# Fourier mixing with experts: fewer expert pieces a step, and the relu between the two copies of the inverse's second stage

## The chip, the cores and the metric

The kernel runs on one core of one Trainium2 chip. The metric is the device time of one execution in microseconds (us).

## What is computed

For each of 8 sequences of 3136 rows with 256 channels: a Fourier transform along the rows, a complex matrix product with soft thresholding, the inverse transform, and then, on the 128 rows with the highest gate score, an expert of two dense layers whose result is added. All of it is float32. Cut to the core:

```python
X = np.fft.rfft(x, axis=1)
Yr = Xr @ w_r - Xi @ w_i + b_r
Yi = Xr @ w_i + Xi @ w_r + b_i
Y* = np.sign(Y*) * np.maximum(np.abs(Y*) - 0.01, 0.0)      # real and imaginary part
y = np.fft.irfft(Y, n=3136, axis=1)
scores = y @ w_gate
for b in range(8):
    top = np.argpartition(-scores[b], 128)[:128]
    ye = np.maximum(y[b, top] @ w1, 0) @ w2
    out[b, top] = y[b, top] + sigmoid(scores[b, top])[:, None] * ye
```

## The kernel before, in words

The transform of 3136 = 98 x 32 is done in two stages each way. The work is cut into T = 100 units (sequence b, group g of frequencies), and one loop over the step t (line 788) writes the order of all engines out by hand; nothing is rescheduled later, each engine runs its list in order. In step t stand, in this order:

- `s2` (forward stage two) of unit t + 1: TensorE products into the bank `px`, on ScalarE the rounded copy `Xh` (L500), on VectorE the rest `Xl` (L501).
- `pair`: one product group `s1` (forward stage one, L440) or `s1i` (inverse stage one, L632) of other sequences, with ScalarE's copy of its result (`at` L443, `ot` L634).
- `turn("pe", "da")`: one move of the router, which finds the 128 rows by eight rounds of counting; its product of a round (L260) writes into the bank `pca`. Placing the rows (L300 to L334) follows.
- `spectral` of unit t (L503): six products into `pcb[:, D:]` (the sum product), ScalarE's copy `ks` (L515), GpSimd's `kb` (ks plus bias, L517), twelve products into `py`, and VectorE's addition of `kb` onto `py` (L521).
- Expert pieces. `ffns` holds two Python generators, `fetch` (L698, gathers the 128 rows) and `ffn` (L707: `prepare` with two transposes and VectorE's and ScalarE's work on gate and rows, 16 first-layer products in 8 pieces of two, 8 combining products in 8 pieces). One `tick` moves each generator by one piece. The number a step is set at line 820.
- A second `pair`, where there is one.
- `s2i` of unit t - 1 (L531, inverse stage two): eight products into `pca[:, :D]` and `pcb[:, :D]` (L549), then for each of the two a ScalarE copy into `ct` (L559) and a VectorE product with the gate's weights that sums up (`junk`, `Csc`, L561). ScalarE copies `pca` while VectorE reads `pcb`, then they change over.
- `shrink` of unit t (L524): ScalarE's relu `r1` of `py` (L526), VectorE's `Y` from `py` and `r1` (L528). `py` has one buffer, so the twelve products of the next step wait for `Y`; the next step's sum product writes the bank `pcb`, from which the second copy reads.

Experts of sequences 0 to 4 may run inside the loop from step 40 on, once the sequence's output is stored; those of 5, 6 and 7 come at step 98 and after. Behind the loop, a list of turns (`work` L855, `fill` L655) mixes the last router's rounds, the last `s1i`, the experts that are left and filler products (L664) that compute nothing.

Of the kernel before, what the change touches and what calls it, by code (L numbers as in the profile page):

```python
# [111 lines left out]
def fourier_moe(ctx: ExitStack, tc: tile.TileContext, x, w_r, w_i, b_r, b_i, wg, w1, w2,  # L112
# [46 lines left out]
    def ld(out, src):  # L159
        nc.sync.dma_start(out=out, in_=src)  # L160
# [35 lines left out]
    def consts_g(k):  # L196
        if k < 3:
            s = slice(8 * k, 8 * k + 8)
            ld(g_sb[:, s, :], t_g[:, s, :])
        else:  # L200
            ld(gt_sb, t_gt)
# [206 lines left out]
    def ld_x(b, i):  # L408
        if i % 2:
            return  # L410
        k = i // 2
        t = (cvs if b < 2 and k > 1 else xts)[k % 2]
        xt[b, k] = t.rearrange("p (h c) d -> p h c d", h=2)
        ld(t.rearrange("p c d -> p (c d)"), x[b, k])
# [106 lines left out]
        nc.vector.tensor_tensor(out=py[:r], in0=py[:r], in1=kb[:r], op=ALU.add)  # L521
        return py, r

    def shrink(b, g, py, r):  # L524
        r1 = pool.tile([128, 2, D], F32, name="r1", bufs=RB)
        nc.scalar.activation(out=r1[:r], in_=py[:r], func=AF.Relu, bias=m2l[:r], scale=1.0)  # L526
        y = pool.tile([128, 2, D], F32, name="Y", bufs=YB)
        nc.vector.scalar_tensor_tensor(out=y[:r], in0=py[:r], scalar=0.0, in1=r1[:r], op0=ALU.min, op1=ALU.add)  # L528
        Y[b, g] = y

    def s2i(b, g):  # L531
        for k in (b, b + 1 if g == G - 1 else b):
            if k not in Cs:
                Cs[k] = Csd[k]
                Csc[k] = pool.tile([128, 32], F32, name="Csc")
                nc.vector.memset(Csc[k][:, NJ - 1:], 0.0)
        if g == G - 1:
            ct[b, g] = pool.tile([128, 2, D], F32, name="ct2", bufs=1)
        elif g % 4 == 0:
            ct[b] = pool.tile([128, 8, D], F32, name="ct", bufs=2)  # L540
        y = Y.pop((b, g))
        p = [t[:, :D] for t in (pca, pcb)]
        if (b, g) == units[T - 1]:
            p = [ps.tile([128, 2, 2 * D], F32, name="px", bufs=1)[:, 0, :D], pcb[:, :D]]
        if g < G - 1:
            for c in range(2):
                for q in range(2):
                    for a in range(2):
                        nc.tensor.matmul(p[q][64 * a:64 * a + 64], gi_sb[64 * q:64 * q + 64, g, c, 64 * a:64 * a + 64], y[64 * q:64 * q + 64, c, :],  # L549
                                         start=(c == 0), stop=(c == 1))  # L550
        else:
            for c in range(2):
                for k in range(2):
                    nc.tensor.matmul(p[k][:64], gti_sb[64 * k:64 * k + 64, c, :], y[64 * k:64 * k + 64, c, :], start=(c == 0), stop=(c == 1))
        o = 2 * (g % 4)
        t = ct[b, g] if g == G - 1 else ct[b]
        for k in (1, 0):
            r, bk, col = (128, b, 2 * g + k) if g < G - 1 else (64, b + k, NJ - 1)
            nc.scalar.copy(out=t[:r, o + 1 - k, :], in_=p[1 - k][:r])  # L559
            junk = pool.tile([128, D], F32, name="junk", bufs=1)  # L560
            nc.vector.tensor_tensor_reduce(out=junk[:r], in0=p[k][:r], in1=wgb[:r], scale=1.0, scalar=0.0,  # L561
                                           op0=ALU.mult, op1=ALU.add, accum_out=Csc[bk][:r, col:col + 1])
        if g == G - 1:
            def store():
                for k in range(2):
                    for q in range(2):
                        ld(Cs[b + k][q, 48] if b + k < B - 1 else Cs[b + k][(N1 - 1) * q], t[q:64:2, k, :])
            stores.append(store)
        elif b == B - 1 and g in (3, 7, 10, 11):
            def store():  # L570
                lo, n = {10: (0, 6), 11: (6, 8)}.get(g, (0, 8))
                for k in (0, 2) if g == 3 else (g // 4,):
                    for q in range(2):
                        ld(Cs[b][1 + 48 * q:49 + 48 * q].rearrange("(j t a) n d -> t (a n) j d", t=3, a=2)[k, :, lo:n], t[q::2, lo:n])
            stores.append(store)
        elif b < B - 1 and g % 4 == 3:
            def store():
                for q in range(2):
                    ld(Cs[b][q, :48].rearrange("(j a) n d -> (a n) j d", a=2)[:, 2 * g - 6:2 * g + 2], t[q::2])
            stores.append(store)  # L580

    def score(b, rep):
        score_ps = banks(b)[2]
        tp = score_ps[:, :N2]
        for q in range(4):
            nc.tensor.matmul(tp[32 * q:32 * q + 32], Csc[b], ident[:, 64 * (q // 2) + q % 2:64 * (q // 2) + 64:2], start=True, stop=True)
        yield "da"
        t = pool.tile([128, 4, 16, 8], F32, name="sct", bufs=1)
        nc.scalar.copy(out=t, in_=tp.rearrange("p (k o c) -> p k o c", k=4, o=1).broadcast_to([128, 4, 16, 8]))
        if b == B - 1:  # L590
            yield "pe"

        def spread():
            v = ps.tile([128, 2, 2 * D], F32, name="s", bufs=1)[:, 0] if b < B - 1 else ps.tile([128, 2 * D], F32, name="py", bufs=1)
            v = v[:, :S // 8]
            for k in range(4):
                nc.tensor.matmul(v[:, N1 * k:N1 * k + N1], t[:, k].rearrange("p m c -> p (m c)"), wq, start=True, stop=True)
            nc.scalar.copy(out=rep, in_=v)
            done["rep"] = b

        if b == B - 1:
            spread()
        else:
            spreads.append(spread)
        while done["rep"] < b:
            yield "db"

    def ld_c(b, i):
        if i % 2 == 0:
            cv[b, i // 2] = cvs[i // 2 % 2]  # L610
            ld(cv[b, i // 2][15:113], Cs[b].rearrange("r m n d -> (r m) n d")[:, 4 * i:4 * i + 8, :])
# [56 lines left out]
    units = [u for b in range(0, B, 2) for u in [(b, g) for g in range(G)] + [(b + 1, g) for g in range(G - 1)]]  # L668
    units.insert(13, units.pop(12))
    T = len(units)  # L670
# [82 lines left out]
    def flush():  # L753
        for f in stores:
            f()
        del stores[:]

    def steady(u):
        return (due(25) if u == 26 else []) + (due(u) if u > 25 else [])
# [28 lines left out]
    for t in range(-1, T):  # L788
        flush()
        for b, i in steady(t + LEAD + 4):  # L790
            ld_x(b, i)
        for u in (t + 3, t + 4):
            if 1 < u < T and (units[u][1] == G - 1) == (u == t + 3):
                ld_a(*units[u])
        for b, i in loads[t] if t >= 0 else ():
            ld_c(b, i)
        if t > T - 3:
            ld_last(*((0, 2) if t == T - 2 else (2, 1)), False)
        if t in (0, 4, 8):
            consts_g(t // 4 + 1)  # L800
        if t in (-1, 1, 4, 9):
            consts_gi((-1, 1, 4, 9).index(t))
        if t == 8:
            consts_b()
        if t in (24, 28, 32, 36):
            consts_moe((t - 24) // 4)
        if 0 <= t + 1 < T:
            s2(*units[t + 1])
        pairs = [(s1, b, i) for b, i in steady(t + LEAD)]
        if t in first:  # L810
            pairs.append((s1, 1, first[t]))
        for _ in plan[t] if t >= 0 else ():
            pairs.append((s1i, *rest.pop(0)))

        def pair():
            if pairs:
                f, b, i = pairs.pop(0)
                f(b, i)

        ticks = 2 + (t % 3 > 0) if t < T - 1 else 0  # L820
        if not pairs and ticks:
            tick(ffns)
            ticks -= 1
        pair()
        turn("pe", "da")
        if 0 <= t < T:
            py, r = spectral(*units[t], lambda: turn("db"))
        else:
            turn("db")
        for b, i in steady(t + LEAD + 2):  # L830
            fold(b, i, nc.gpsimd)
        if t + 2 in first and first[t + 2] > 1:
            fold(1, first[t + 2], nc.gpsimd)
        done["t"] = t
        for _ in range(ticks):
            tick(ffns)
        if t == T - 1:
            shrink(*units[t], py, r)
        if spreads and not pairs:
            spreads.pop(0)()  # L840
        pair()
        if 0 <= t - 1 < T:
            b, g = units[t - 1]
            s2i(b, g)
            if g == G - 1 - b % 2:
                done["s2i"] = b
        if 0 <= t < T - 1:
            shrink(*units[t], py, r)
    t = T

    def ready():
# [68 lines left out]
```

## Time and profile before

| | |
|---|---|
| median of 3 runs | 682.16 us (681.22 to 682.57) |
| profiled execution, its own time | 682.17 us |
| its span (first to last instruction) | 680.4 us |
| TensorE busy (products) | 645.3 us, 95% |
| VectorE busy | 443.3 us, 65% |
| ScalarE busy | 371.6 us, 55% |
| GpSimd busy | 283.7 us, 42% |
| mean granted TensorE clock | 0.990 |
| moved to and from memory | 253 GB/s over the span |

Matmuls are pipelined: a product's row has a modelled length, longer than the distance to the next one, so that a short wait of TensorE lies inside a busy row. Waits are therefore read from the starts of successive rows rather than from the busy share.

### The profile page before, as it was taken

The page shows a single profiled execution, that of the slowest core. Times are in us where ns is not written, and L with a number is a line of the kernel's source. Part 1 is how long each engine was busy: PE and PEld are TensorE (multiplying, and loading weights), DVE is VectorE, ACT ScalarE, POOL GpSimd, SP SyncE. Part 2 cuts the span into 40 slices and gives each one's busy share as a digit, 9 for nine tenths or more (in the row PEclk, how much of TensorE's full clock was granted, in tenths as well). Part 3 has the DMA queues.
Part 4 walks back from the last instruction along what each step waited for, and adds up shares of the span by engine and source line. Part 5 has one row for each costly group of instructions (what it writes and reads, how often), then busy time and mean ns, then how long its engine had stood idle before and what let it go on. Part 6 is the DMA issues. An engine that isn't in the chain of part 4 may idle for free.

```text
span 680.4 us, 20492 instructions
## 1 busy us (share of the span) xinstructions
PE 645.3 (95%) x8371; PEld 481.4 (71%) x8371; DVE 443.3 (65%) x1386; ACT 371.6 (55%) x672; POOL 283.7 (42%) x241
## 2 busy tenths in 40 slices
PE   6699989999999999999999999999999999999996
PEld 2467666777777777777777777768777877776765
DVE  3346556687588765776677756677578766887550
ACT  3245555566656666655564665556655555555340
POOL 1257655555555555454344454544354222222101
PEclk9789999999999999999999999999999999999998
DMA  8998767698989898979669668897958556787760
GB/s 309 321 367 258 273 207 237 228 333 269 342 260 328 276 329 281 314 236 317 221 196 300 195 255 264 292 321 224 288 183 256 160 164 207 212 285 240 235 196 25
DMA packets 73982, 173.53 MB, mean 255 GB/s; under 512 B 4896, under 2 KB 58626, under 8 KB 60418
## 3 DMA queue, kind: packets, MB, share of 16 engines
q1 hardware_dynamic: 72704, 169.87, 75.7%
q0 software_dynamic: 896, 2.17, 1.0%
q8 instruction: 66, 1.08, 0.6%
q10 hardware_dynamic: 288, 0.18, 0.1%
q14 instruction: 28, 0.23, 0.1%
HBM read 93.10 MB, written 79.17 MB: 253 GB/s over the span
## 4 chain that ended last, share of the span: by engine, by line
PE 65%; DVE 11%; ACT 8%; issue 6%; POOL 6%; DMA 3%; POOLq 0%; ACTq 0%; DVEq 0%
PE pca L549 9%; PE s L632 6%; PE py L233 6%; PE px L488 5%; PE s L440 5%; POOL kb L517 5%; PE py L234 5%; PE py L235 4%; PE pcb L233 3%; PE m L384 3%; DVE junk L561 3%; ACT r L526 3%; PE m L400 3%; PE pcb L235 2%; PE pcb L234 2%
## 5 line engine op out<-in xcount | busy, mean ns | idle before, releaser
L517 POOL TENSOR_TENSOR kb<-ks,bias 128x512 f32<-128x512 f32 x100 | 127.6, 1276 | 317.3 <-ACT ks L515 221.8
L421 POOL TENSOR_TENSOR sd<-xt 113x512 f32<-113x512 f32 x104 | 130.4, 1277 | 27.5 <-DMA xt<-in_x 27.5
L521 DVE TENSOR_TENSOR py<-py,kb 128x512 f32<-128x512 f32 x100 | 69.9, 699 | 72.6 <-POOL kb L517 70.3
L559 ACT COPY ct<-pca 128x256 f32<-128x256 f32 (+1 forms) x99 | 37.0, 374 | 132.0 <-PE pcb L549 120.3
L501 DVE TENSOR_TENSOR Xl<-px,Xh 128x768 fp32r<-128x768 f32 x100 | 95.8, 958 | 12.5 <-ACT Xh L500 12.5
L549 PE MATMUL pca<-Y,gi_sb 64*64 64x256 f32 x760 | 101.8, 386 | 1.6 <-DVE pca L255 0.4
L549 PE MATMUL pcb<-Y,gi_sb 64*64 64x256 f32 x768 | 103.0, 386 | 0.0
L528 DVE SCALAR_TENSOR_TENSOR Y<-py,r 128x512 f32<-128x512 f32 x100 | 69.1, 691 | 44.9 <-ACT r L526 44.8
L488 PEld LDWEIGHTS px<-g_sb,av 64*64 64x64 f32 x3072 | 77.8, 134 | 14.2 <-DVE Xl L501 2.2
L500 ACT CAST Xh<-px 128x768 fp32r<-128x768 f32 x100 | 80.1, 801 | 11.2 <-PE px L488 11.2
L488 PE MATMUL px<-g_sb,av 64*64 64x96 f32 x3072 | 82.8, 244 | 2.0 <-DVE Xl L501 2.0
L634 ACT COPY ot<-s 128x1024 f32<-128x1024 f32 x58 | 59.6, 1028 | 36.5 <-PE s L632 36.1
L549 PEld LDWEIGHTS pca<-Y,gi_sb 64*64 64x64 f32 x760 | 46.5, 132 | 36.9 <-issue 10.0
L526 ACT ACTIVATE r<-py,m2l 128x512 f32<-128x512 f32 x100 | 69.2, 692 | 4.3 <-DVE py L521 4.3
L561 DVE CUSTOM_DVE_ANT_0 junk<-pcb,wgb 128x256 f32<-128x256 f32 (+1 forms) x100 | 42.2, 422 | 43.2 <-PE pcb L549 38.7
L233 PE MATMUL pcb<-wsh,Xh 128*128 128x256 f32 x200 | 65.5, 327 | 2.5 <-ACT ct L559 2.5
L440 PE MATMUL s<-sd,w 64*64 64x512 f32 x480 | 64.8, 599 | 2.9 <-ACT ot L634 1.4
L233 PE MATMUL py<-wnh,Xh 128*128 128x256 f32 x200 | 61.6, 308 | 4.2 <-DVE Y L528 3.3
L632 PE MATMUL s<-cv,wi_sb 64*64 64x512 f32 x464 | 61.9, 598 | 0.4 <-DMA cv<-Cs 0.4
L443 ACT COPY at<-s 128x1024 f32<-128x1024 f32 x58 | 60.1, 1035 | 2.6 <-PE s L440 2.6
L234 PE MATMUL pcb<-wsh,Xl 128*128 128x256 f32 x200 | 56.1, 280 | 0.0
L234 PE MATMUL py<-wnh,Xl 128*128 128x256 f32 x200 | 55.9, 280 | 0.0
(182 smaller groups left out, 1341.1 us busy)
## 6 DMA issues: line engine op xcount, KB each, us to landing
xt<-in_x SPq DMA_DIRECT2D x28, 1024.0 KB
Cs<-ct SPq DMA_DIRECT2D x48, 512.0 KB
av<-As SPq DMA_DIRECT2D x46, 512.0 KB
cv<-Cs SPq DMA_DIRECT2D x30, 784.0 KB
out<-ot SPq DMA_DIRECT2D x30, 784.0 KB
As<-at SPq DMA_DIRECT2D x28, 784.0 KB
cv<-in_x SPq DMA_DIRECT2D x4, 1024.0 KB
xt<-Cs SPq DMA_DIRECT2D x1, 1568.0 KB
```

The costliest lines, as they stand in the source:

```text
L233: nc.tensor.matmul(out, wh, mh, start=start, stop=False)
L234: nc.tensor.matmul(out, wl, mh, start=False, stop=False)
L421: eng.tensor_tensor(out=f[:113, k], in0=t[:113, 0], in1=t[:113, 1], op=op)
L440: nc.tensor.matmul(p[64 * c:64 * c + 64, r, :], w[64 * r:64 + NH * r, v, :], f[64 * r:64 + NH * r], start=(k == 0), stop=(k == len(parts[0 ...
L488: nc.tensor.matmul(o[:, :, N2 * j:N2 * j + N2], a[64 * p:64 * p + 64, j, g % 4, 128 * h + 64 * q:128 * h + 64 * q + 64], g_sb[64 * p:64 * ...
L500: nc.scalar.copy(out=vh, in_=v)
L501: nc.vector.tensor_tensor(out=vl, in0=v, in1=vh.bitcast(F32), op=ALU.subtract)
L517: nc.gpsimd.tensor_tensor(out=kb[:r], in0=ks[:r].broadcast_to([r, 2, D]), in1=bias[:r], op=ALU.add)
L521: nc.vector.tensor_tensor(out=py[:r], in0=py[:r], in1=kb[:r], op=ALU.add)
L526: nc.scalar.activation(out=r1[:r], in_=py[:r], func=AF.Relu, bias=m2l[:r], scale=1.0)
L549: nc.tensor.matmul(p[q][64 * a:64 * a + 64], gi_sb[64 * q:64 * q + 64, g, c, 64 * a:64 * a + 64], y[64 * q:64 * q + 64, c, :], start=(c == ...
L632: nc.tensor.matmul(p[64 * c:64 * c + 64, r, :], wi_sb[64 * r:64 + NH * r, b // (B - 1), 15 * c:15 * c + 64], f[64 * r:64 + NH * r, 4 * c + ...
```

## The change

Two things. At each step but the last one, one expert piece fewer is given out: 1, 2, 2 in turn, not 2, 3, 3. And the relu of unit t is issued inside `s2i` of unit t - 1, after the first of the two copies and VectorE's first product, so that ScalarE's order is copy, relu, copy, not copy, copy, relu. Where a step has no inverse before it, or is the last, the relu stays in `shrink`.

```diff
-    def shrink(b, g, py, r):
+    def relu(py, r):
         r1 = pool.tile([128, 2, D], F32, name="r1", bufs=RB)
         nc.scalar.activation(out=r1[:r], in_=py[:r], func=AF.Relu, bias=m2l[:r], scale=1.0)
+        return r1
+
+    def shrink(b, g, py, r, r1=None):
+        r1 = r1 or relu(py, r)
         y = pool.tile([128, 2, D], F32, name="Y", bufs=YB)
...
-    def s2i(b, g):
+    def s2i(b, g, between=None):
...
                                            op0=ALU.mult, op1=ALU.add, accum_out=Csc[bk][:r, col:col + 1])
+            if k and between:
+                r1 = between()
...
+        return r1 if between else None
...
-        ticks = 2 + (t % 3 > 0) if t < T - 1 else 0
+        ticks = 1 + (t % 3 > 0) if t < T - 1 else 0
...
-            s2i(b, g)
+            r1 = s2i(b, g, (lambda: relu(py, r)) if t < T - 1 else None)
...
-            shrink(*units[t], py, r)
+            shrink(*units[t], py, r, r1 if t > 0 else None)
```

The order of ScalarE in one step, before (L526 is the relu, L559 the copies, L500 the rounded copy of the next unit):

```order
L515 COPY ks<-pcb 128x256
L559 COPY ct<-pca 128x256
L559 COPY ct<-pcb 128x256
L526 ACTIVATE r_603<-py,m2l 128x512
L500 CAST Xh<-px 128x2x6x64
L443 COPY at<-s 128x2x512
L515 COPY ks<-pcb 128x256
```

and with the change:

```order
L515 COPY ks<-pcb 128x256
L563 COPY ct<-pca 128x256
L526 ACTIVATE r_600<-py,m2l 128x512
L563 COPY ct<-pcb 128x256
L500 CAST Xh<-px 128x2x6x64
L443 COPY at<-s 128x2x512
L515 COPY ks<-pcb 128x256
```

The relu and the copy of `pcb` have changed places. What each waits for: the relu for VectorE's addition into `py`, the copy for VectorE's product on `pcb`.

TensorE late in the loop, from the last of the twelve products to the inverse, in a step in which the last router counts, before:

```order
L233 MATMUL py<-wdh,Xh 128x256
L234 MATMUL py<-wdh,Xl 128x256
L235 MATMUL py<-wdl,Xh 128x256
L549 MATMUL pca<-Y,gi_sb 64x256 x2
L549 MATMUL pcb<-Y,gi_sb 64x256 x2
```

and with the change (L384 is an expert's first layer, L553 the inverse):

```order
L233 MATMUL py<-wdh,Xh 128x256
L234 MATMUL py<-wdh,Xl 128x256
L235 MATMUL py<-wdl,Xh 128x256
L384 MATMUL m<-xT,w1s 128x128 x2
L553 MATMUL pca<-Y,gi_sb 64x256 x2
L553 MATMUL pcb<-Y,gi_sb 64x256 x2
```

The expert of sequence 4 was over by step 88 and now runs through most of the last ten steps; of the 60 steps from 40 on, nearly all have a piece now.

TensorE at the very end, from the placing of the last sequence's rows (L334) on, before (L664 is filler, L359 the transposes of the last expert, the L384 and L400 behind them its two layers):

```order
L334 MATMUL pca<-row,hot 128x34
L334 MATMUL pca<-neg,hot 128x34
L334 MATMUL pca<-row,hot 128x34
L334 MATMUL pca<-neg,hot 128x34
L400 MATMUL py<-w2s,hh 128x256 x3
L664 MATMUL s<-wsh 128x512 x8
L359 MATMUL m<-ident,xe 128x128 x2
L384 MATMUL s<-xT,w1s 128x128 x8
L384 MATMUL m<-xT,w1s 128x128 x8
L400 MATMUL px<-w2s,hh 128x256 x8
```

and with the change:

```order
L334 MATMUL pca<-row,hot 128x34
L334 MATMUL pca<-neg,hot 128x34
L334 MATMUL pca<-row,hot 128x34
L334 MATMUL pca<-neg,hot 128x34
L384 MATMUL py<-xT,w1s 128x128 x4
L384 MATMUL m<-xT,w1s 128x128 x8
L400 MATMUL py<-w2s,hh 128x256 x8
L671 MATMUL s<-wsh 128x512 x8
L359 MATMUL m<-ident,xe 128x128 x2
L384 MATMUL s<-xT,w1s 128x128 x8
L384 MATMUL m<-xT,w1s 128x128 x8
L400 MATMUL px<-w2s,hh 128x256 x8
```

Twelve first-layer and eight combining products of the expert of sequence 6 now stand between the placing and the last expert, where three combining products stood. In all, three combining pieces of expert 4 and the `prepare` of expert 5 have moved from the loop to behind it.

## Rows read from the trace of the kernel before

**Rows 1.** Page, part 1: busy time and share of the span.

```profile
PE 645.3 (95%) x8371; PEld 481.4 (71%) x8371; DVE 443.3 (65%) x1386; ACT 371.6 (55%) x672; POOL 283.7 (42%) x241
```

**Rows 2.** Stretches, additions L521 alone: length, VectorE busy (count), TensorE clock, DMA share, GB/s.

```profile
40.76:127.69 86.93, 11.89 (x17) 1.00 0.75 254
127.69:269.33 141.64, 16.81 (x25) 1.00 0.88 297
```

**Rows 3.** Timeline, ScalarE, one early step: start, length, line, operation [idle before <- releaser].

```profile
62.10 0.37 ACT L559 COPY ct<-pca 128x256 f32<-128x256 f32 x1 [1.69 <-PE pcb L549]
62.85 0.37 ACT L559 COPY ct<-pcb 128x256 f32<-128x256 f32 x1 [0.38 <-DVE Csc L561]
63.12 0.69 ACT L526 ACTIVATE r<-py,m2l 128x512 f32<-128x512 f32 x1
63.70 0.80 ACT L500 CAST Xh<-px 128x768 fp32r<-128x768 f32 x1
64.38 1.04 ACT L443 COPY at<-s 128x1024 f32<-128x1024 f32 x1
65.28 0.41 ACT L515 COPY ks<-pcb 128x256 f32<-128x256 f32 x1
```

**Rows 4.** Timeline, VectorE, the same step.

```profile
61.79 0.70 DVE L521 TENSOR_TENSOR py<-py,kb 128x512 f32<-128x512 f32 x1 [1.58 <-POOL kb L517]
...
63.31 0.08 DVE L561 DVE_READ_ACCUMULATOR2_ANT Csc<- 128x1 f32 x1
63.84 0.69 DVE L528 SCALAR_TENSOR_TENSOR Y<-py,r 128x512 f32<-128x512 f32 x1 [0.45 <-ACT r L526]
...
67.07 0.70 DVE L521 TENSOR_TENSOR py<-py,kb 128x512 f32<-128x512 f32 x1 [1.58 <-POOL kb L517]
```

**Rows 5.** Timeline, GpSimd, the same step.

```profile
65.77 1.27 POOL L517 TENSOR_TENSOR kb<-ks,bias 128x512 f32<-128x512 f32 x1 [1.54 <-ACT ks L515]
```

**Rows 6.** Timeline, TensorE, the same step (forward stage two, sum product, the twelve).

```profile
61.88 0.84 PE L488 MATMUL px<-g_sb,av 64*64 64x96 f32 x32
...
63.52 0.39 PE L233 MATMUL pcb<-wsh,Xh 128*128 128x256 f32 x1
...
64.68 0.36 PE L233 MATMUL py<-wnh,Xh 128*128 128x256 f32 x1 [0.20 <-DVE Y L528]
```

**Rows 7.** Timeline, TensorE, a step with router product and pieces (sum product, twelve, pieces).

```profile
302.69 0.36 PE L233 MATMUL pcb<-wsh,Xh 128*128 128x256 f32 x1
...
303.50 0.36 PE L233 MATMUL py<-wnh,Xh 128*128 128x256 f32 x1
...
304.98 1.46 PE L400 MATMUL m<-w2s,hh 128*128 128x256 f32 x6
```

**Rows 8.** Timeline, TensorE, a router step without a piece (first of the twelve, inverse).

```profile
598.88 0.35 PE L233 MATMUL py<-wnh,Xh 128*128 128x256 f32 x1
...
600.62 0.43 PE L549 MATMUL pca<-Y,gi_sb 64*64 64x256 f32 x2
```

**Rows 9.** Timeline, VectorE, the same step as rows 8.

```profile
600.40 0.16 DVE L255 TENSOR_TENSOR pca<-digits,pca 128x1 uint32<-128x1 uint32 x1
```

**Rows 10.** Timeline, TensorE, router products behind a `prepare`: the fourth and the last.

```profile
452.09 0.40 PE L260 MATMUL pca<-digits,n 128*128 128x15 f32 x2 [0.72 <-DVE Csc L561]
...
625.72 0.20 PE L300 MATMUL pca<-tm,mask 98*64 98x98 bf16 x1 [1.24 <-DVE Csc L561]
```

**Rows 11.** Timeline, TensorE, the end: placing, filler, last expert.

```profile
660.40 0.31 PE L334 MATMUL pca<-row,hot 98*128 98x34 f32 x2
...
662.40 2.19 PE L664 MATMUL s<-wsh 128*128 128x512 f32 x8
665.68 0.41 PE L359 MATMUL m<-ident,xe 128*128 128x128 f32 x2 [1.09 <-DMA xe<-out,idx]
...
669.98 2.10 PE L384 MATMUL m<-xT,w1s 128*128 128x128 f32 x16
```

**Rows 12.** Stretches at the end: length, busy of PE, PEld, DVE, ACT, POOL, clock, DMA.

```profile
666.60:669.80 3.20, 3.19 (x16) 3.19 (x17) 0.29 (x2) 0.20 (x1) 0.00 (x0) 0.54 0.03 8
```

## The prediction

> **What bounds the kernel now.** I read the busy shares first, then the starts of successive rows within single steps, then the end. TensorE's products are busy for 95% of the span and no other engine for more than 65% [rows 1]. That looks like a kernel bound by TensorE alone, in which an order on ScalarE would be worth nothing. But a row's length is modelled, so I compare starts.
>
> An early step shows a ring. The second copy starts at 62.85, the relu 0.27 us later, `Xh` 0.58 after that, `at` 0.68, `ks` 0.90 [rows 3]; `kb` follows 0.49 after `ks` [rows 5]; the next addition 1.30 after `kb`, and an addition stands 1.06 before its own step's second copy (61.79 to 62.85) [rows 3, 4]. The sum is 5.28 us, and one addition and the next lie 67.07 - 61.79 = 5.28 apart [rows 4]: the step lasts as long as the ring does. TensorE fits into it with a wait: its twelve products start at 64.68, when `Y` (63.84 to 64.53) has been written [rows 4, 6], 1.16 after the sum product's start at 63.52, where the same six products take 302.69 to 303.50 = 0.81 in a step that is full [rows 6, 7]. So 0.35 of each such step is waiting. There are 17 additions from 40.76 to 127.69, that is 16 steps, of 86.93 / 16 = 5.43 us on average [rows 2].
>
> In a later step with a router product and an expert piece there is no such wait: the twelve take 303.50 to 304.98 = 1.48 [rows 7]. In a router step without a piece they take 598.88 to 600.62 = 1.74 [rows 8]: the inverse writes `pca` and waits for the router's last small VectorE operation on that bank, at 600.40 and 0.16 long [rows 9]. The 0.26 is lost. Third, behind each `prepare` the next router product waits for VectorE (0.72 in the fourth, 1.24 in the last [rows 10]), since VectorE has the expert's two extra operations ahead of the inverse's.
>
> **The relu between the copies.** Removed: nothing. Moved: 98 relus, one place earlier on ScalarE. The relu needs the addition, which ends at 61.79 + 0.70 = 62.49; with an estimate of 0.06 for the handover (`Y`'s end at 64.53 to the twelve products' start at 64.68 is 0.15 [rows 4, 6], `kb`'s end at 67.04 to the addition at 67.07 is 0.03 [rows 4, 5]), it starts at 62.55, behind the first copy (62.10, 0.37 long) [rows 3, 4], and not at 63.12. The second copy follows 0.58 later, as `Xh` follows the relu now: 63.13, not 62.85. `Xh` follows a copy by 0.27: 63.40, not 63.70. The ring becomes 0.76 (addition to relu) + 0.58 + 0.27 + 0.68 + 0.90 + 0.49 + 1.30 = 4.98, so 0.30 less. `Y` then waits for VectorE itself, whose last `Csc` ends at 63.39 [rows 4], so it starts near 63.45, 0.39 earlier, and the twelve products do not wait for it. TensorE's own path through the step is the same 5.28 less the 0.35, so 4.93: both limits agree. **16 steps x 0.30 = 4.8 us.** Bounds: nothing, if TensorE has another wait behind this one; 16 x 0.35 = 5.6 if the ring gives way wholly. I take the ring, because its links sum to the period.
>
> What is queued behind the moved relu: the second copy, and behind that the next sum product, which writes the same bank. The copy now ends at 63.22 and the product starts at 63.52, 0.30 later [rows 3, 6]; with the change the copy ends at 63.50, and the 0.30 is nearly used up. I book nothing for it here, since a router product stands ahead of the sum product in most later steps. The Trainium skill, page "PSUM — Partial Sum Buffer", section on bank collisions, says that two engines must be kept off one bank even when they touch different columns, and even when both only read. By that the sum product cannot overtake the late copy; were the addition late in every step as well, the sum would turn positive, which is the third rival below.
>
> In router steps without a piece the same shift moves VectorE's chain (relu, `Y`, `Xl`, the router's small operations) 0.3 earlier and so covers the 0.26.
>
> **Fewer pieces a step.** No product is added or removed in the experts (8 x 24 products, each doubled in the trace); they stand in other steps. By the order, 13 router steps without a piece lose 0.26 each (seven from 127.69 to 269.33, of 25 steps there [rows 2], two or so in the middle, four near the end); in most of the later ones a piece now stands where the wait was, and the relu covers the others. **13 x 0.26 = 3.4.** A dozen more router steps have another product group as partial cover; I take a third, **1.0**; bounds 0 and 3.1.
>
> Six `prepare`s stand in the loop, five after. The last one's wait, 1.24, goes; in the five others the addition comes 0.3 earlier and the wait shrinks by that: **1.24 + 1.5 = 2.7.** Bounds: 1.2 (the wait only follows VectorE) and 5 x 0.72 + 1.24 = 4.8.
>
> The loop is also shorter by what moves behind it: three combining products, 1.39 / 3 = 0.46 each [rows 7], and a `prepare` of some 0.3: **1.7 off the loop.**
>
> **The end.** From the placing (660.40) to the last expert's transposes (665.68) there are 5.28 us now, in which TensorE does 0.8 of placing, three combining products, fillers, and waits 1.09 for the gathered rows [rows 11]. With the change there stand 0.9 of placing, 12 first-layer products (each twice 2.10 / 16 = 0.13 [rows 11], so 3.1), 8 combining products (8 x 0.46 = 3.7), and the fillers (8 x 0.22 = 1.8): 9.5, so 4.2 more, and the gather is hidden. In exchange TensorE does not stand idle ahead of the last expert: its first half ran at a mean granted clock of 0.54 [rows 12], near the lower of the two levels, 16 products in 3.2 instead of 2.1, so 1.1 comes back. Ahead of the placing the expert's gate work stands in front of the last scoring copy on ScalarE (later by up to 1), while the counting rounds hold less other work (shorter by 1 or more); I take 0 of bounds +1.0 and -1.5. **Net +3.1.**
>
> The sum, against the profiled execution's 682.17 (the median is 682.16, so nothing has to be shifted): 682.2 - 4.8 - 3.4 - 1.0 - 2.7 - 1.7 + 3.1 = **671.7 us**.
>
> **Rivals.**
> *TensorE is the bound after all.* The 0.26 in router steps is its own change of operands and remains; only the ring and the prepares gain. For it: 95% [rows 1]. Against: 1.48 and 1.74 for the same twelve products [rows 7, 8]. 682.2 - 4.8 - 2.7 - 1.7 + 3.1 = 676.1. Chance 0.15.
> *Transfers give it back.* From 127.69 to 269.33 the DMA engines are busy for 0.88 at 297 GB/s [rows 2]; steps that are 5% shorter ask for 0.92. If loads come late there, half of the ring's gain and the router steps' gain go: 682.2 - 2.4 - 2.7 - 1.7 + 3.1 = 678.5. Chance 0.10.
> *The copy behind the relu becomes the wait.* Place: the first sum product of the 40 or so steps without a router product ahead of it. Price: the second copy moves from 1.06 to 1.34 after the addition, 0.28, so 11.2 us if the slack of 0.30 [rows 3, 6] isn't there, and the ring's gain is lost on the way. It decides where the addition starts later against the first copy than the 0.31 ahead of it that it has here (61.79 against 62.10). 682.2 + 11.2 - 4.4 - 2.7 - 1.7 + 3.1 = 687.7: slower. Against it: `Y`, not the copy, is what the twelve products wait for [rows 6]. Chance 0.08.
> *The end eats it.* If the loop gains half (6) and the end costs both of its upper bounds (+1.0, and no clock back, 1.1): 682.2 - 6.0 - 1.7 + 5.2 = 679.7, up to 682 if the rounds lengthen too. Chance 0.09, a third of it faster by less than can be told.
> *More than forecast.* The prepares' waits vanish (4.8), the dozen steps give 3.1 and the rounds 1.5: 682.2 - 4.8 - 3.4 - 3.1 - 4.8 - 1.7 + 1.6 = 666.0. Chance 0.08.
>
> **The numbers.** The forecast has 0.50. A difference under 0.2% (1.4 us) can't be told from none. Faster: 0.50 + 0.15 + 0.10 + 0.08 and a third of 0.09, 0.86, less 0.01 for the edge of the second rival: 0.85. Same: 0.06. Slower: 0.08 and a little from the end, 0.09. The range reaches below 666 by the bounds not yet used, to 664.5, and above the rivals that end faster, to 681.0; slower cases and a few others stay outside.
>
> **What would show it.** Right: steps of 4.95 to 5.05 before 127 us; the twelve products at 1.48 in all router steps; `Y` waiting for VectorE, not for the relu; the placing of the last rows some 10 to 13 us earlier, and 9 us from it to the last transposes with the clock at 1.0 behind it. Wrong: the sum product waiting for the second copy in many steps; waits for loads at the first products of a pair; early steps still above 5.2, which would mean that the ring was not the limit.

## The result, and the profile after

| | before | with the change |
|---|---|---|
| median of 4 runs | 682.28 us (681.22 to 682.57) | 671.83 us (669.25 to 674.36) |
| ratio | | 0.9849, 95% interval 0.9803 to 0.9896 |
| profiled execution, its span | 682.17, 680.4 us | 669.25, 667.5 us |

The forecast was 671.7. The changed kernel's runs lie in two pairs, 669.25 and 670.15 at a mean granted clock of 0.994 and 0.992, and 673.51 and 674.36 at 0.982; the experiments take that up. The page's first part, after:

```profile
PE 633.3 (95%) x8375; PEld 473.4 (71%) x8375; DVE 436.9 (65%) x1386; ACT 365.9 (55%) x672; POOL 284.7 (43%) x241
```

The shares are those of [rows 1] to within a hundredth, although 12.9 us are gone: the busy share told nothing about this change. An early step, ScalarE, then VectorE, then TensorE (timeline of the kernel after; columns as in [rows 3]):

```profile
66.69 0.37 ACT L563 COPY ct<-pca 128x256 f32<-128x256 f32 x1 [1.59 <-PE pcb L553]
67.27 0.69 ACT L526 ACTIVATE r<-py,m2l 128x512 f32<-128x512 f32 x1 [0.22 <-DVE py L521]
67.86 0.36 ACT L563 COPY ct<-pcb 128x256 f32<-128x256 f32 x1
68.11 0.81 ACT L500 CAST Xh<-px 128x768 fp32r<-128x768 f32 x1
...
66.48 0.70 DVE L521 TENSOR_TENSOR py<-py,kb 128x512 f32<-128x512 f32 x1 [1.58 <-POOL kb L517]
...
68.00 0.69 DVE L532 SCALAR_TENSOR_TENSOR Y<-py,r 128x512 f32<-128x512 f32 x1
...
67.13 1.04 PE L440 MATMUL s<-sd,w 64*64 64x512 f32 x8
68.28 0.38 PE L233 MATMUL pcb<-wsh,Xh 128*128 128x256 f32 x1
...
69.09 0.28 PE L233 MATMUL py<-wnh,Xh 128*128 128x256 f32 x1
```

The links answer to [rows 3, 4, 6]. The relu starts 0.79 after the addition's start (it waits for it), the second copy 0.59 later, `Xh` 0.25 after that: 1.63 from the addition to `Xh`, where it was 1.06 + 0.27 + 0.58 = 1.91. `Y` follows the last `Csc`, and the twelve products run on without a wait for it. The next step's forward stage starts at 71.49, this one's at 66.47: 5.02, where it was 5.28. The sum product now starts 0.06 after the second copy's end (68.22); before it had 0.30. So it waits for that copy now. It starts 68.28 - 67.13 = 1.15 behind the first product of the pair ahead of it, and before it was 63.52 [rows 6] - 62.54 = 0.98:

```profile
62.54 1.04 PE L440 MATMUL s<-sd,w 64*64 64x512 f32 x8
```

The early step is therefore still bound by the ring, whose links now sum to 0.79 + 0.59 + 0.25 + 0.70 + 0.90 + 0.48 + 1.31 = 5.02. TensorE waits 0.17 a step, at the sum product and no longer at the twelve.

Where the time went, by stages cut at the first product of a step's forward stage, with the steps numbered from 0 at 40.76 us in the kernel before, one less than the loop's t (all engines; length, busy times with counts, clock, DMA share, GB/s). Before, the two stages that no row has shown so far:

```profile
269.33:618.05 348.72, 342.80 (x4624) 262.23 (x4620) 244.89 (x784) 199.54 (x368) 142.92 (x116) 1.00 0.76 245
618.05:680.40 62.35, 53.64 (x423) 39.48 (x415) 28.05 (x130) 20.76 (x35) 7.50 (x7) 0.97 0.54 170
```

After:

```profile
125.69:263.22 137.53, 137.15 (x1983) 102.50 (x1979) 102.99 (x336) 87.56 (x161) 72.37 (x59) 1.00 0.90 304
263.22:601.88 338.66, 334.01 (x4614) 256.89 (x4610) 241.20 (x783) 195.06 (x368) 142.59 (x115) 1.00 0.78 255
601.88:667.50 65.62, 56.72 (x437) 39.19 (x429) 28.04 (x130) 20.95 (x35) 8.50 (x8) 0.99 0.50 163
```

Step 0 starts at 39.88 instead of 40.76, steps 0 to 15 take 125.69 - 39.88 = 85.81 instead of 86.93 [rows 2], steps 16 to 40 take 137.53 instead of 141.64, steps 41 to 96 take 338.66 instead of 348.72, and the end takes 65.62 instead of 62.35: -0.9 - 1.1 - 4.1 - 10.1 + 3.3 = -12.9.

The large surprise is the third and fourth number. They come with a sign that the trace of before had held all along. A step late in the loop, before (VectorE) and after (VectorE, TensorE):

```profile
302.66 0.69 DVE L528 SCALAR_TENSOR_TENSOR Y<-py,r 128x512 f32<-128x512 f32 x1 [0.45 <-ACT r L526]
```

```profile
288.85 0.68 DVE L532 SCALAR_TENSOR_TENSOR Y<-py,r 128x512 f32<-128x512 f32 x1
...
290.20 0.28 PE L233 MATMUL py<-wnh,Xh 128*128 128x256 f32 x1
...
291.60 0.61 PE L384 MATMUL m<-xT,w1s 128*128 128x128 f32 x4
```

Before, `Y` ended at 303.35, and the first of the twelve products stood at 303.50 with 0.36 [rows 7]: the same 0.15 behind `Y` and the same length as in the early steps [rows 4, 6]. It had waited. After, `Y` has been ready for 0.67, the first product takes 0.28, and the twelve take 1.40, not 1.48. The 1.48 that I had taken for a step without a wait contained one, of 0.08. In the trace of before the first of the twelve follows `Y` by at most 0.16 and is longer than 0.30 in 76 of 99 steps; after, in two.

**Theory A**: the ring addition - relu - `Y` - twelve products set the length of nearly every step, and moving the relu is the whole gain. **Theory B**, the prediction's: it set the 16 early steps, and later gains come from pieces that stand where TensorE waited.

### The profile page after: what moved, and what is told of

It reads as the page before. It is cut to its first block, busy times and chain, and to the rows that moved or that the text cites. A ratio compares the mean times of both kernels' runs of the same rounds, so it can differ in the third digit from the quotient of the medians.

```text
span 667.5 us, 20596 instructions
## 1 busy us (share of the span) xinstructions
PE 633.3 (95%) x8375; PEld 473.4 (71%) x8375; DVE 436.9 (65%) x1386; ACT 365.9 (55%) x672; POOL 284.7 (43%) x241
## 4 chain that ended last, share of the span: by engine, by line
PE 74%; issue 6%; ACT 5%; POOL 5%; DVE 5%; DMA 4%; SPq 1%; POOLq 0%; ACTq 0%; DVEq 0%
PE pca L553 11%; PE px L488 7%; PE s L639 7%; PE s L440 6%; PE py L235 6%; PE py L233 6%; PE py L234 6%; PE pcb L233 4%; POOL kb L517 3%; PE pcb L234 3%; PE pcb L235 3%; PE m L384 3%; PE pca L260 3%; DMA at<-As 2%; PE m L400 2%
## 5 line engine op out<-in xcount | busy, mean ns | idle before, releaser
L521 DVE TENSOR_TENSOR py<-py,kb 128x512 f32<-128x512 f32 x100 | 70.0, 700 | 79.0 <-POOL kb L517 79.0
L553 PE MATMUL pcb<-Y,gi_sb 64*64 64x256 f32 x768 | 102.9, 386 | 0.1
L553 PE MATMUL pca<-Y,gi_sb 64*64 64x256 f32 x760 | 101.7, 386 | 1.0 <-DMA gi_sb<-t_gi 1.0
L500 ACT CAST Xh<-px 128x768 fp32r<-128x768 f32 x100 | 82.1, 821 | 12.8 <-PE px L488 11.0
L526 ACT ACTIVATE r<-py,m2l 128x512 f32<-128x512 f32 x100 | 69.4, 694 | 7.2 <-DVE py L521 6.8
L553 PEld LDWEIGHTS pca<-Y,gi_sb 64*64 64x64 f32 x760 | 46.6, 132 | 35.4 <-issue 11.3
L233 PE MATMUL py<-wnh,Xh 128*128 128x256 f32 x200 | 56.0, 280 | 0.1
L235 PE MATMUL pcb<-wsl,Xh 128*128 128x256 f32 x200 | 55.9, 280 | 0.0
```

Of the source, the lines that this page charges most:

```text
L233: nc.tensor.matmul(out, wh, mh, start=start, stop=False)
L235: return nc.tensor.matmul(out, wh, ml, start=False, stop=stop).ins
L500: nc.scalar.copy(out=vh, in_=v)
```

## The experiments

Stage lengths of all profiled executions, from the starts of steps 1, 10, 16, 41 and 97 and the span (us; steps 1 to 9 are 9 steps, 16 to 40 are 25, 41 to 96 are 56). "Alone" means with the other half as before:

| kernel | steps 1-9 | 10-15 | 16-40 | 41-96 | end |
|---|---|---|---|---|---|
| before | 49.14 | 32.44 | 141.64 | 348.72 | 62.35 |
| changed | 47.14 | 32.30 | 137.53 | 338.66 | 65.62 |
| changed, again | 46.96 | 33.71 | 138.07 | 339.39 | 70.42 |
| relu alone | 46.86 | 31.94 | 137.98 | 340.63 | 60.67 |
| pieces alone | 49.26 | 33.10 | 141.65 | 345.13 | (see there) |
| relu ahead of both copies | 49.12 | 32.40 | 141.70 | 341.28 | 65.54 |
| before, one copy more | 51.60 | 34.04 | 148.89 | 363.01 | 61.47 |
| relu alone, one copy more | 47.44 | 32.62 | 140.67 | 344.81 | 61.88 |
| gaps filled | 46.91 | 33.85 | 137.89 | 338.63 | 65.74 |
| gaps filled, short end | 46.90 | 31.69 | 137.78 | 339.71 | 64.36 |
| gaps filled, short end, again | 47.61 | 31.72 | 137.63 | 338.43 | 64.40 |
| relu alone, again | 48.05 | 32.32 | 137.65 | 340.67 | 60.50 |
| relu alone, two pieces a step | 46.73 | 31.23 | 137.80 | 343.95 | 60.98 |

### The two halves, each alone

The relu alone is the changed kernel with one line as before, the pieces alone the kernel before with that line changed:

```diff
-        ticks = 1 + (t % 3 > 0) if t < T - 1 else 0
+        ticks = 2 + (t % 3 > 0) if t < T - 1 else 0
```

> The relu between the two copies, expert pieces two or three a step as before. Theory A (the wait for Y is in nearly every step of the kernel before: there the first of the twelve products took 0.36 us, as after a wait, in most steps, and 0.28 in the changed kernel): the relu alone removes it everywhere, so early stage 86 us, the stage up to the first expert 137.5, the loop with experts some 8 us shorter, the end as before; 667 to 670 us. Theory B (the ring limits the early steps only, and later waits are filled by the pieces): the loop with experts keeps its length but for 1.5 behind the prepares; 673 to 676 us.

> One or two pieces a step, relu behind both copies as before. Theory A: the wait for Y stays in most steps, a piece behind the twelve products hides only the wait of the inverse for VectorE in the last router steps; the loop is 1.7 shorter by what moves behind it and one prepare's 1.2, the end is 3.3 longer: 680.5 to 683 us. Theory B: the loop with experts becomes some 8 us shorter by the pieces: 675 to 678 us.

Measured: the relu alone 669.03 us (666.47 to 669.97), ratio 0.9796 (0.9781 to 0.9810); in a second comparison 669.33, 0.9792 (0.9765 to 0.9819). The pieces alone 688.33 us (684.04 to 699.27), ratio 1.0064 (1.0041 to 1.0087): slower, by less than a hundredth. The product of the two ratios is 0.986, near the change's 0.985: the halves add up, and one of them is a loss. Much of that loss goes with the granted clock: the three executions of the pieces alone at 0.988 to 0.989 took 684.0 to 685.8 us, the four at 0.982 or less 688 to 699.

By stages: the relu alone has the changed kernel's lengths up to step 41 to within half a us, and 8.1 of the 10.1 behind it. The starts of TensorE's rows show where: up to the second of the twelve products, which is the wait for `Y`, the relu alone wins 2.7 of its 3.7 us in steps 16 to 40 and 5.4 of its 8.1 in steps 41 to 96. A further 1.6 and 1.4 come at the inverse, which waits for VectorE in the kernel before. So `Y` is two thirds to three quarters of the gain there, and not all of it. With the pieces alone the steps 16 to 40 take 141.65, as before to 0.01; no expert piece stands there in either kernel. Its steps 41 to 96 are 3.6 shorter, but five combining products of the expert of sequence 4 (5 x 0.46 = 2.3 [rows 7]) have only moved to step 97 and later. That leaves 1.3. The last `prepare` and its wait of 1.24 [rows 10] lie behind step 96 (618.05) in the kernel before as well, so they are no part of the 3.6. Theory A, which expected little more than work that moves, is near that; B's 675 to 678 falls. That it came out above A's 680.5 to 683 too is the end's doing, below.

### The relu ahead of both copies

```diff
         t = ct[b, g] if g == G - 1 else ct[b]
+        r1 = between() if between else None
         for k in (1, 0):
...
-            if k and between:
-                r1 = between()
```

> The changed kernel with the relu ahead of both copies. Theory A: in early steps the addition ends only after the inverse, so both copies stand behind the relu, the next sum product waits for the second copy, and a step takes 5.3 us as in the kernel before instead of 5.02; in later steps the addition is done before the inverse and the relu costs the copies nothing. 675 us (673 to 677), with the loss before 125 us alone. Rival: the second copy decides in all steps without a router product, 0.3 each in 35 steps: 682 us. Rival: ScalarE's order no longer matters once the relu is ahead of the second copy: 672 us.

Measured: 681.4 us, ratio 0.9971 (0.9950 to 0.9993); its six executions at a clock of 0.990 to 0.992 took 677.9 to 679.7, about 9 more than the changed kernel's at that clock; in the six others the clock fell (below). ScalarE in an early and in a later step (timeline):

```profile
68.64 0.69 ACT L526 ACTIVATE r<-py,m2l 128x512 f32<-128x512 f32 x1 [2.19 <-DVE py L521]
69.23 0.36 ACT L564 COPY ct<-pca 128x256 f32<-128x256 f32 x1
69.48 0.38 ACT L564 COPY ct<-pcb 128x256 f32<-128x256 f32 x1
69.74 0.82 ACT L500 CAST Xh<-px 128x768 fp32r<-128x768 f32 x1
...
213.91 0.69 ACT L526 ACTIVATE r<-py,m2l 128x512 f32<-128x512 f32 x1 [2.19 <-DVE py L521]
```

TensorE at each of these two steps:

```profile
69.92 0.39 PE L233 MATMUL pcb<-wsh,Xh 128*128 128x256 f32 x1 [0.21 <-ACT ct L564]
...
215.38 0.39 PE L260 MATMUL pca<-digits,n 128*128 128x15 f32 x2 [0.18 <-DVE Csc L566]
```

The addition starts at 67.85; to the relu 0.79, then 0.59, 0.25 and 0.26 to `Xh`: 1.89, as the 1.91 of before. With the other links that is the old ring, and its stages up to step 41 are those of before to within 0.1. So the middle place is not just "earlier": ahead of both copies, the first copy, which has time while the addition runs, goes into the ring. My expectation for the later steps failed: the addition is not done before the inverse there (213.91 waits for it), so 4.2 were lost in steps 16 to 40 and 2.6 behind. In the router's steps the wait is at the router product, which needs `Csc`, VectorE's work behind the late first copy (215.38). The 678.6 lies between A and the rival, whose mechanism is in sight in the early steps: the sum product waits for the second copy and starts 0.06 after its end (69.86 to 69.92), as it does in the changed kernel, but later in the step (1.25 behind the pair's first product, not 1.15). The Trainium skill, page "PSUM — Partial Sum Buffer", section on bank collisions, says that two engines must not use one bank at once, even on different columns; the trace agrees in that TensorE never enters `pcb` before the copy has left it (0.04 us after it at the nearest).

### One copy more ahead of the relu

```diff
         r1 = pool.tile([128, 2, D], F32, name="r1", bufs=RB)
+        dm = pool.tile([128, D], F32, name="dm", bufs=1)
+        nc.scalar.copy(out=dm[:r], in_=wgb[:r])
         nc.scalar.activation(out=r1[:r], in_=py[:r], func=AF.Relu, bias=m2l[:r], scale=1.0)
```

> The kernel before with one copy more on ScalarE (128x256, from a constant, nobody reads it) right ahead of every relu; by the distance of the two copies in the trace some 0.26 us each. Theory A (the wait for Y is in nearly every step): each of the some 70 steps whose twelve products waited for Y becomes longer by 0.26, so 14 to 20 us, about 700 us. Theory B (the ring limits the 16 early steps only): 4 us, 687 us. Rival C (what counts is how much ScalarE has to do): the same loss here and in the next run.

> The same copy ahead of every relu in the kernel with the relu between the copies and pieces as before. Theory A: the copy fits between the first copy and the end of the addition in early steps, and into the 0.3 to 0.5 that Y is now ahead in later steps: 0 to 2 us, 669 to 671 us. Rival C: as much as in the kernel before.

Measured: 715.68 us, ratio 1.0484 (1.0458 to 1.0511), in the kernel before; 682.52 us, 0.9995 (0.9978 to 1.0012), with the relu alone. Both contain an error of mine: the constant arrives late, and the first copy waited 7.5 and 6.1 us for it, once. The stages in the table leave that out. ScalarE in the kernel before with the copy:

```profile
71.27 0.37 ACT L561 COPY ct<-pcb 128x256 f32<-128x256 f32 x1 [0.37 <-DVE Csc L563]
71.54 0.41 ACT L526 COPY dm<-wgb 128x256 f32<-128x256 f32 x1
71.85 0.70 ACT L528 ACTIVATE r<-py,m2l 128x512 f32<-128x512 f32 x1
...
76.86 0.37 ACT L561 COPY ct<-pcb 128x256 f32<-128x256 f32 x1 [0.38 <-DVE Csc L563]
```

The copy pushes the relu back by 0.31, and the step grows from 5.28 to 5.59. In the other stages each step grows by (148.89 - 141.64) / 25 = 0.29 and (363.01 - 348.72) / 56 = 0.26. Together 24.0 in these 90 steps, 77 times the 0.31 and more than the 14 to 20 of theory A: the kernel before waited for `Y` in most of its steps, as the 76 rows say. With the relu between the copies the same copy costs 0.06, 0.11 and 0.07 a step (0.58 / 9, 2.69 / 25, 4.18 / 56): 7.5 in the 90 steps instead of 24.0. Rival C falls. A's "0 to 2" was too low, though the twelve products still wait for `Y` in one step of 99 only: by the starts of TensorE's rows, 3.0 of the 7.5 are lost at the inverse, 1.8 at the router product and most of the rest at the sum product, which now starts within 0.06 of the second copy's end in 40 steps of 100, where it was 12 without the added copy. So other waits stand close behind the one that the relu's place has removed.

### The changed kernel again, and its end

> The changed kernel once more, beside the parts of it. Its four runs lay between 669.25 and 674.36 us, so both theories expect 670 to 674, and the difference between its profiles tells how much of the spread is load waits and how much is the granted clock.

Measured: 672.1 us (669.56 to 678.53), ratio 0.9831 (0.9805 to 0.9856). The median lies in the expected 670 to 674, three of the five runs don't. The profiled execution is the longest, 678.53. Its end took 70.42, not 65.62. TensorE in the changed kernel around the last scoring (timeline, first profile):

```profile
617.91 0.44 PE L359 MATMUL m<-ident,xe 128*128 128x128 f32 x2 [0.98 <-DVE ye L403]
...
619.91 1.13 PE L604 MATMUL py<-wq,sct 128*128 128x98 f32 x8 [0.54 <-ACT sct L596]
...
621.62 0.60 PE L384 MATMUL py<-xT,w1s 128*128 128x128 f32 x3 [0.52 <-ACT rep L605]
```

The same place in stretches, first profile, then the longer execution:

```profile
616.88:621.88 5.00, 2.96 (x26) 2.13 (x26) 2.21 (x10) 1.54 (x4) 1.01 (x1) 1.00 0.63 209
621.88:636.88 15.00, 14.38 (x104) 8.96 (x107) 10.38 (x58) 5.17 (x6) 0.96 (x1) 1.00 0.59 168
```

```profile
620.35:625.35 5.00, 3.48 (x24) 2.10 (x21) 2.36 (x11) 1.42 (x4) 1.00 (x1) 0.91 0.75 250
625.35:638.00 12.65, 12.16 (x59) 11.84 (x57) 5.20 (x30) 1.68 (x3) 0.96 (x1) 0.50 0.49 130
```

The same waits in the longer execution, and the clock just before and after its fall:

```profile
622.32 0.44 PE L359 MATMUL m<-ident,xe 128*128 128x128 f32 x2 [0.98 <-DVE ye L403]
624.32 1.91 PE L604 MATMUL py<-wq,sct 128*128 128x98 f32 x8 [0.55 <-ACT sct L596]
624.25:624.50 0.25, 0.18 (x1) 0.18 (x2) 0.00 (x0) 0.01 (x1) 0.00 (x0) 0.96 0.77 221
624.50:638.00 13.50, 13.01 (x62) 12.69 (x62) 5.20 (x30) 1.68 (x3) 0.96 (x1) 0.50 0.52 142
```

With one or two pieces a step the expert of sequence 5 is not prepared in the loop. Its `prepare` and the waits for `ye`, `sct` and `rep` now follow closely on each other. In one execution the granted clock then stays at 1.00. In another it falls to the lower level around the end of the second wait (624.5), ahead of the third (626.80), and stays there for 13.5 us; the end is 4.8 longer. To see whether these waits are what lets it fall, I filled them with products that compute nothing:

```diff
             if item[0] == B - 1:
                 idle(8)
+            if item[0] == B - 3:
+                idle(5)
...
+        if t == T + 1:
+            idle(2)
         work(us, t < T + 2)
         if threads:
             fill(us if t < T + 5 else min(us, 1.0))
+            if t == T:
+                idle(3)
```

> The changed kernel with ten filler products more around the last scoring, where its TensorE waits three times within 5 us (0.98 for ye, 0.54 for sct, 0.52 for rep). Theory: these waits, which fewer pieces have moved to that place, let the granted clock fall in some executions (0.50 for some 13 us in the profile of 678.53 us, 1.00 throughout in that of 669.25); filled, it never falls, all runs lie between 668.5 and 670.5 us and the median is 669.5. Rival: the spread comes from load waits; then the runs spread over 669 to 678 as before, median 672.

Measured: 670.2 us (668.93 to 672.61), ratio 0.9814 (0.9788 to 0.9840). The fillers lengthen the end by 0.1 (65.74). Not all runs fell into the expected 2 us (668.5 to 670.5): two are longer. The profiled one, 671.82, had its clock at 1.00 until TensorE's last products, but not earlier: behind two waits of the edge unit it fell to the lower level for 3.4 us, and steps 10 to 15 took 33.85.

```profile
101.06 0.75 PE L496 MATMUL px<-gt_sb,at 64*64 64x192 f32 x10 [0.81 <-DMA at<-As]
101.60:105.00 3.40, 3.40 (x20) 1.71 (x10) 0.96 (x1) 1.81 (x2) 0.00 (x0) 0.50 0.00 0
```

So "filled, it never falls" holds for the filled place alone. Nor is the fall at the end, 4.8 in the one profile that can be compared, the only cause of spread: the relu alone, with no mean clock below 0.986, lay between 665.2 and 670.7. Which cause is the larger stays open. Counted over all runs: with this end and unfilled gaps (the changed kernel, the pieces alone, the relu ahead of both) 14 of 28 executions had a mean clock of 0.982 or less; with the gaps filled, or with the expert of sequence 5 prepared in the loop, none of 31 (the two kernels with the added copy are left out of this count, because the clock falls at their early wait, to a mean of 0.66 from 46 to 56 us). That these 14 fell at the same place is seen in two profiles and concluded from the mean for the rest. One is the longer execution above, the other that of the pieces alone: after waits of 0.98 and 0.55 its clock was at 0.50 for 40 us of its end, so its end is not compared here.

```profile
634.00:674.40 40.40, 39.81 (x158) 23.65 (x158) 14.82 (x81) 9.83 (x12) 1.97 (x2) 0.50 0.37 109
```

The last edit also shortens the fillers ahead of the last expert, which cover the gather's way:

```diff
             if item[0] == B - 1:
-                idle(8)
+                idle(2)
```

> As the run before, and two filler products instead of eight ahead of the last expert. In the changed kernel the gather was issued at 649.85 us and the fillers stood from 652.4 to 654.44; in the kernel before the transposes came 2.9 us after their gather, so the rows are there at about 652.7 and 1.5 of the fillers' 2.0 cover nothing: 668.0 us. Rival: with fewer fillers the clock is at 0.50 in the last expert, 16 products in 3.2 instead of 2.1, so 670 us or more.

> The changed kernel with its three waits around the last scoring filled and two filler products instead of eight ahead of the last expert, once more: 667 to 669 us; it and the relu alone do not differ by more than 0.2%.

Measured: 668.09 us (667.25 to 668.98), ratio 0.9780 (0.9760 to 0.9800), and again 668.19, 0.9794 (0.9778 to 0.9810). First the changed kernel's TensorE and GpSimd at the end, then this one's:

```profile
652.40 2.20 PE L671 MATMUL s<-wsh 128*128 128x512 f32 x8
654.44 0.38 PE L359 MATMUL m<-ident,xe 128*128 128x128 f32 x2
...
649.85 0.96 POOL L348 DMA_INDIRECT xe<-out,idx  x1 [5.94 <-PE m L384]
```

```profile
653.56 0.81 PE L671 MATMUL s<-wsh 128*128 128x512 f32 x2
654.21 0.38 PE L359 MATMUL m<-ident,xe 128*128 128x128 f32 x2
...
651.02 0.96 POOL L348 DMA_INDIRECT xe<-out,idx  x1 [5.95 <-PE m L384]
```

From the gather to the transposes it is 3.19 instead of 4.59, without a wait, and the last expert's clock stayed at 1.00. The end is 1.4 shorter than with the gaps filled alone.

### Does spreading the pieces bring anything?

With two pieces in every step, and the relu between, the pieces lie wider than before, but nothing more moves behind the loop:

```diff
-        ticks = 2 + (t % 3 > 0) if t < T - 1 else 0
+        ticks = 2 if t < T - 1 else 0
```

> The relu between the copies and two expert pieces in every step: pieces are spread wider than before, but the work behind the loop stays what it was before the change. Theory (with the relu moved, there is no wait left that a piece could fill, and the end alone pays for 1, 2, 2): the same as the relu alone within 0.2%, 668 to 670 us, with no fall of the granted clock at the end. Rival (spreading itself hides waits behind the prepares): 666 to 667 us.

> The relu alone once more, on the same chip as the two others of this call: 667 to 670 us, and a narrower spread than the changed kernel's 669 to 678, since the end keeps its clock.

Measured: 668.9 us (667.66 to 671.62), ratio 0.9803 (0.9782 to 0.9825), beside 669.33 (665.20 to 670.73) for the relu alone. No difference, as the theory said; the relu alone spread wider than I had written. In the profile of two a step one load came late:

```profile
596.03 1.34 PE L639 MATMUL s<-cv,wi_sb 64*64 64x512 f32 x8 [2.39 <-DMA cv<-Cs]
597.30 0.61 PE L260 MATMUL pca<-digits,n 128*128 128x15 f32 x2
```

Step 95 waits 2.39 for it, 0.37 in the kernel before and 1.09 with the relu alone; the 64x512 products behind the wait take 1.34 instead of 1.09, and the granted clock had gone down to 0.50 there as well (from 596.8 to 600). The changed kernel has no such wait in these steps, so faster steps alone don't explain it.

## Why the prediction was right, and where it was not

The number was right, 671.7 against 671.83, and the direction; the account behind it was half right. By stages, forecast and measured (profiled execution): steps 0 to 15, -4.8 and -1.1; steps 16 to 40, -1.82 (7 x 0.26) and -4.1; steps 41 to 96, -5.44 (6 x 0.26 + 1.0 + 1.5 + 3 x 0.46) and -10.1; from step 97 on, +1.56 (3.1 less the last `prepare`, 0.3, and its wait, 1.24, which stand there) and +3.3; the start, 0 and -0.9. That makes 10.5 and 12.9. The median of the runs then stands 2.6 us above the profiled execution, because two of the four had a mean clock of 0.982 and not 0.992; that it fell at the end is seen in other profiles, not in theirs. The forecast knew nothing of this. Two errors met, and that the forecast came within 0.2 us is luck.

- **The ring.** Right in its links and in the early steps: 4.98 was forecast for the early step, 5.02 measured; most of the 0.04 is the relu's handover, 0.09 behind the addition instead of 0.06. The step that failed is "in a later step ... there is no such wait: the twelve take ... 1.48". I compared one step with another of the same kernel that waited as well. 1.40 is what they take; the sign was there, a first product of 0.36 and 0.15 behind `Y`. That wait, booked with nothing after step 15, is 2.7 and 5.4 us in the two later stages (relu alone).
- **16 x 0.30.** The steps 1 to 9 gave 2.0 of the expected 2.7. By the rows the twelve products' wait for `Y` shrank by 4.4 there, but the sum product, which now waits for the second copy, took back 2.45. Step 0 gave back the 0.9 that its start was earlier: it waited 1.03 for a constant's load. The edge unit in steps 10 and 11 waited 0.87 and 0.80 for its rows, 0.28 before. So the rival "transfers give it back" acted, but in the first 100 us, not in the busy stretch that I had named:

```profile
45.33 0.43 PE L553 MATMUL pca<-Y,gi_sb 64*64 64x256 f32 x2 [1.03 <-DMA gi_sb<-t_gi]
...
99.28 0.54 PE L496 MATMUL px<-gt_sb,at 64*64 64x192 f32 x4 [0.87 <-DMA at<-As]
100.62 0.70 PE L496 MATMUL px<-gt_sb,at 64*64 64x192 f32 x9 [0.80 <-DMA at<-As]
```

- **Fewer pieces, 13 x 0.26 and 1.0.** The pieces' part failed. Without the relu they change nothing in steps 16 to 40, where none stands, and bring at most 1.3 behind (3.6 less the 2.3 that moved). With the relu moved they find no wait to fill: steps 41 to 96 take 338.66 against 340.63 of the relu alone, 2.0 less, where 2.3 have moved out. The relu's part held: with the relu alone the inverse's waits shrink by 1.6 in steps 16 to 40, where 7 x 0.26 = 1.8 was booked. It is nearer 0.16 in most of them, and there are more than seven. The 0.26 compared an inverse with a piece: behind the last of the twelve the inverse stands 0.21 when it waits for nothing, a piece 0.12.
- **The prepares, 2.7.** Too high: with the relu alone the waits behind the first five sum to 2.11 where they were 3.04, 0.9 less and not 1.5, and the last one is 1.00, not 1.24. In the changed kernel the last one did leave its place, but it came back at the scoring, 0.98 for `ye`, and the fifth `prepare` now waits as well, 1.65 for `ye` at 553.47.
- **The end, +3.1.** Near in sum, 3.3, but that is luck too. From the placing to the last transposes 8.88 instead of 5.28, +3.6 where I had 4.2; the last expert 1.7 faster at a full clock where I had 1.1; the part ahead of the placing +1.3 where I had 0, with two more of the moved combining products in it. The 1.7 isn't the change's. In the relu alone TensorE still waits for the gathered rows ahead of the last expert, and its clock stays at 1.00:

```profile
651.66 0.41 PE L359 MATMUL m<-ident,xe 128*128 128x128 f32 x2 [1.07 <-DMA xe<-out,idx]
651.66:656.06 4.40, 3.88 (x33) 3.64 (x34) 0.76 (x3) 0.80 (x2) 0.00 (x0) 1.00 0.10 32
```

All five profiles with such a wait (1.07 to 1.12) other than that of the kernel before show 1.00 there and 13.0 to 13.1 us from the transposes to the end of the span. The 0.54 of [rows 12], with 14.7, belongs to that one execution. Against the relu alone the changed kernel's end is 5.0 longer.
- **The rivals.** "TensorE is the bound after all" falls with the added copy: a TensorE that is the bound would not have lost 24 us. "The copy behind the relu becomes the wait" is what happens in the early steps with the relu ahead of both copies; between them it happens too, in 12 steps of 100, eleven of them before 125 us, at 0.17 in a plain step instead of the 0.28 of that rival. Most later steps have a router product ahead of the sum product, and there the copy is done in time. "The end eats it" is what the pieces' half did: 3 to 4 us of the relu's 13 to 14.

## What to carry to other kernels

An engine's busy share of 95% and a "full" step of the same kernel are no proof that it isn't waiting: look at the distance between the last input's end and the first product, and at a first row longer than its neighbours. Among instructions that several engines hand round, the best place for one is behind what has time anyway and ahead of what hasn't; up to step 40 both neighbouring places gave the old step. Spreading filler work paid only where a wait was left to fill, and what it pushed behind the loop was paid in full; of the versions run, the relu alone (669 us) and the changed kernel with its end mended (668 us) both beat the change and don't differ measurably.

## What the runs showed of the hardware that I had not expected

Two profiles show TensorE's granted clock falling around the last scoring to the lower of its two levels. It fell around the end of the second of two waits, of 0.98 and 0.55 us (at 624.5, the wait ending at 624.32, and at 633.9, the wait ending at 634.10), and stayed down for 13.5 us in one (the changed kernel) and 40 in the other (the pieces alone), while TensorE was busy nearly throughout (13.01 of 13.50 and 39.81 of 40.40). In the changed kernel's first profile the same waits, 0.98 and 0.54, went by at 1.00. By the mean clock, 14 of 28 executions with these waits fell (0.982 or less). Filling the waits with products that compute nothing cost 0.1 us, and none of 15 executions had a mean as low. Two shorter falls, of 3.4 and some 3.5 us, stood behind waits for loads (0.81 in the kernel with the gaps filled, 2.39 with two pieces a step); waits of 0.87 and 0.80 in the changed kernel's first profile brought none. So the same waits in the same program may or may not be followed by a fall; what decides between the two, no run here shows.
